# Two heads on 96 neighbouring partitions, and unit 1's gap rows sent by ScalarE

## The chip, the cores and the metric

The kernel runs on one core of a Trainium2 chip. The core has TensorE (PE, matrix products, with weight loads shown as PEld), VectorE (DVE), ScalarE (ACT), GpSimd (POOL) and SyncE (SP), which here only issues transfers. Sixteen DMA engines move data between memory and the core's 128-partition on-chip memory. The metric is the device time of one execution in microseconds (us), as the median of several runs.

## The reference

Two computations follow each other. The first is a gated linear recurrence for 4 batches, 8 heads, 768 steps and a head size of 48:

```
f = 1 / (1 + exp(-f_logit))
for t in range(S):
    state = f[:, :, t, :, None] * state + einsum('bhd,bhe->bhde', k[:, :, t], v[:, :, t])
    y[:, :, t] = einsum('bhd,bhde->bhe', q[:, :, t], state)
```

Its result, with the 8 heads side by side (8 x 48 = 384 columns, 4 x 768 = 3072 tokens), goes through a two-layer network: `h = x @ w_in` (384 to 2048), `g = where(h > 0, h, exp(min(h, 0)) - 1)`, `out = g @ w_out` (2048 to 384). q, k, v and f_logit are float32; w_in and w_out come as 8-byte floating point numbers, so each of their elements is twice as large in memory and is turned into float32 on the chip.

## The kernel before

**Units, pairs and halves.** The 3072 tokens are cut into 12 units of 256, three per batch. q, k and f lie with head elements on partitions and tokens innermost. The 8 heads are 4 pairs; in each half of 64 partitions one head of the pair takes 48 partitions and 16 stay over. Before the change the 48 rows stand first in each half (partitions 0 to 47 and 64 to 111, `HALF`, L403) and the 16 over are behind them (48 to 63 and 112 to 127).

**Rows of the network.** The network wants its 384 input rows as three blocks of 128. Three pairs give 96 rows each; the fourth pair's 96 rows are cut into six strips of 16, which go into the 16 partitions over in each half of the three blocks: the gap rows. In unit 0 matrix products write them in place (`first_outputs`, L719, with the zero-padded tiles `padded_v` and `padded_s`). From unit 1 on `carried` (L693) copies the products to `xt` on ScalarE and sends the six strips to their places with six small transfers (L717), issued by SP. `fetch` (L500) lays w_in's rows to match: two transfers for the 48-row parts and two for the 16-row parts of each piece (L515, L516).

**Attention of a unit.** `load` (L417) issues f, k and q as two transfers each, one per half, and v as one. In unit 0 the second half's transfers are issued by ScalarE, the rest by SP. `blank` (L430) fills the tiles of the first two units beforehand, so that the partitions over hold neutral values. `gates` (ScalarE, GpSimd) and `decays` (L588: a scan and a reciprocal on VectorE and products on GpSimd, for each of the 4 pairs) turn f into products of decays and scale k and q. `transposed` turns k (TensorE, L616) and ScalarE copies it to `kn` (L620); `advance` (L660, matmul L668), `step` (L624, VectorE), `scores` (L637), `mask` (L653), `outputs` (L674) and `carried` follow for chunks of 64 tokens.

**Weights.** There are 16 pieces, 8 of w_in and 8 of w_out, fetched into 7 places in turn (`AHEAD`). Each goes through `split` (two VectorE instructions, L530 and L534), `lower` (ScalarE, L540, about 1.9 us) and `merge` (VectorE, L548), and `merge` issues the fetch for the place that it frees.

**Order.** Each engine's instructions stand in an order written out by hand (a manual schedule). The start is listed one call after another (L970 to L1013); from there a plan says at which step T of the network which part of the attention, which merge and which load is issued (`at_step`, L760; the numbers `A1`, `D2`, `A2`, `D3`, `A3`). An even step T is one block of first-layer products (`up`, L864, psH) and an odd one a block of second-layer products, two blocks behind (`down`, L894, psM). `warm` (L961) puts products whose result nobody uses (psW) on TensorE at fixed places. The units from 2 on use a scheme with seven products in place of eight for 2 by 2 blocks (L819, L916), with sums on GpSimd (L883).

**Queues.** Transfers start in the order in which SP or ScalarE issues them, and up to eight completion counters are used in turn by all of them, whichever engine issues.

## Time and profile before

| | |
|---|---|
| Median of 14 runs | 578.52 us (576.31 to 579.71) |
| The profiled execution, its own time | 578.4 us |
| Its span | 576.7 us |
| Mean granted clock of TensorE | 0.987 |
| TensorE busy | 556.1 us (96%) |
| VectorE busy | 437.0 us (76%) |
| ScalarE busy | 235.3 us (41%) |
| GpSimd busy | 271.0 us (47%) |
| DMA queue of SP | 36144 packets, 49.07 MB |
| DMA queue of ScalarE | 912 packets, 0.79 MB |

The profile is of one execution. The views used below: the chain of work that ended last (start, duration, what), the timeline of an engine (start, busy time, engine, line, operation, tile written and read, how many; in brackets how long the engine stood before it, and for what), the transfers by queue (packets, MB, share of the DMA engines) and the view by stretches of time (stretch and its length; busy time and number of instructions of PE, PEld, DVE, ACT and POOL; then the granted clock of TensorE, the busy share of the DMA engines, and GB/s). All times are counted from the start of the span. L with a number is a line of the kernel.

### The profile page before, as it was taken

What the parts mean: (1) busy time and instruction counts of PE and PEld (TensorE: products, weight loads), DVE (VectorE), ACT (ScalarE), POOL (GpSimd) and SP (SyncE); (2) the same over time, 40 slices, a digit from 0 to 9 for tenths busy, and PEclk for the clock granted to TensorE, in tenths of its full rate; (3) what the DMA queues carried; (4) which work ended last, traced back from release to release, by engine and by line L of the source; (5) the groups of instructions that cost most, each with busy time, mean ns of one, the idle gap of its engine ahead of it and who ended that gap; (6) DMA issues with size and microseconds to landing.
All of it is one profiled execution on the core that took longest, in us unless ns stands there. A gap on an engine that the chain in (4) does not pass through costs nothing.

```text
span 576.7 us, 15424 instructions
## 1 busy us (share of the span) xinstructions
PE 556.1 (96%) x6236; PEld 505.4 (88%) x6236; DVE 437.0 (76%) x838; ACT 235.3 (41%) x437; POOL 271.0 (47%) x559
## 2 busy tenths in 40 slices
PE   6599999999999999999999999999999999999994
PEld 2376777777999999999999999999999999999994
DVE  7799659674896896897897887788878888745542
ACT  3357855443433343343343343443343253343331
POOL 6320014851466366267257257356357348325332
PEclk9979999999999999999999999999999999999998
DMA  8999980034014216216206207207207201201001
GB/s 180 231 237 266 191 221 0 2 83 90 2 42 109 81 42 131 84 30 145 84 15 159 85 8 166 84 8 167 83 7 168 85 3 60 84 2 35 28 2 34
DMA packets 37138, 50.94 MB, mean 88 GB/s; under 512 B 4257, under 2 KB 27841, under 8 KB 37057
## 3 DMA queue, kind: packets, MB, share of 16 engines
q1 hardware_dynamic: 36144, 49.07, 35.6%
q8 instruction: 51, 0.84, 0.6%
q10 hardware_dynamic: 912, 0.79, 0.6%
q14 instruction: 31, 0.25, 0.2%
HBM read 44.04 MB, written 4.72 MB: 85 GB/s over the span
## 4 chain that ended last, share of the span: by engine, by line
PE 89%; DVE 4%; issue 2%; ACT 1%; DMA 1%; POOL 1%; DVEq 0%; ACTq 0%; POOLq 0%
PE psH L819 32%; PE psM L916 31%; PE psH L864 7%; PE psM L894 7%; PE psS L647 3%; PE psY L684 2%; PE psY L704 2%; PE psW L965 2%; PE psT L616 2%; PE psU_a L668 1%; PE psY L743 1%; DVE o L926 1%; DMA f<-in_f_logit_dram 1%; DVE state L631 1%; DVE u L926 1%
## 5 line engine op out<-in xcount | busy, mean ns | idle before, releaser
L819 PE MATMUL psH<-xt,wi 128*128 128x128 f32 (+1 forms) x960 | 177.3, 294 | 0.0
L883 POOL TENSOR_TENSOR sums<-gg 128x128 f32<-128x128 f32 x160 | 69.7, 456 | 180.6 <-DVE gg L873 142.2
L851 ACT ACTIVATE gg<-hh 128x512 f32<-128x512 f32 x80 | 50.5, 631 | 223.9 <-POOL sums L883 130.9
L819 PEld LDWEIGHTS psH<-xt,wi 128*128 128x128 f32 x960 | 136.0, 192 | 0.7
L819 PE MATMUL psH<-xt,area 128*128 128x128 f32 x640 | 110.7, 275 | 0.0
L819 PEld LDWEIGHTS psH<-xt,area 128*128 128x128 f32 x640 | 96.9, 192 | 4.0
L916 PE MATMUL psM<-area,sums 128*128 128x192 f32 x480 | 91.1, 326 | 0.0
L828 DVE TENSOR_TENSOR hh<-psH,u 128x256 f32<-128x256 f32 x80 | 33.6, 420 | 68.8 <-ACT u L826 68.8
L597 DVE RECIPROCAL p<-f 128x256 f32<-128x256 f32 x48 | 84.1, 1753 | 1.7
L916 PEld LDWEIGHTS psM<-area,sums 128*128 128x128 f32 x480 | 80.2, 190 | 0.0
L916 PE MATMUL psM<-wo,gg 128*128 128x192 f32 x320 | 68.2, 336 | 0.0
L852 ACT ACTIVATE gg<-gg 128x512 f32<-128x512 f32 x96 | 60.6, 631 | 3.0
L873 DVE SCALAR_TENSOR_TENSOR gg<-gg,hh 128x512 f32<-128x512 f32 x80 | 56.5, 706 | 1.5 <-ACT gg L852 1.5
L916 PEld LDWEIGHTS psM<-wo,gg 128*128 128x128 f32 x320 | 50.2, 191 | 1.9
L841 DVE TENSOR_TENSOR hh<-psH,u43h 128x256 f32<-128x256 f32 (+1 forms) x160 | 49.7, 352 | 2.7
L598 POOL TENSOR_TENSOR k<-k,f 128x256 f32<-128x256 f32 x48 | 35.5, 740 | 28.3 <-DVE f L594 21.7
L883 POOL TENSOR_TENSOR sums<-gg,sums 128x128 f32<-128x128 f32 x80 | 43.4, 543 | 6.3
L864 PE MATMUL psH<-xt,wi 128*128 128x256 f32 x192 | 45.0, 385 | 0.7 <-DMA xt<-xt 0.7
L894 PE MATMUL psM<-wo,gg 128*128 128x384 f32 x128 | 44.2, 489 | 0.0
L864 PEld LDWEIGHTS psH<-xt,wi 128*128 128x128 f32 x192 | 36.3, 193 | 8.6 <-issue 2.3
L883 POOL TENSOR_TENSOR sums<-sums,gg 128x128 f32<-128x128 f32 x80 | 40.0, 500 | 0.0
L841 DVE TENSOR_TENSOR u43h<-psH,hh 128x256 f32<-128x256 f32 x80 | 33.5, 419 | 7.7 <-PE psH L819 7.7
(96 smaller groups left out, 752.8 us busy)
## 6 DMA issues: line engine op xcount, KB each, us to landing
area<-in_moe_w_out_dram SPq DMA_DIRECT2D x8, 768.0 KB, 8.2
again<-in_moe_w_in_dram SPq DMA_DIRECT2D x16, 384.0 KB, 4.2
again<-in_moe_w_out_dram SPq DMA_DIRECT2D x16, 384.0 KB, 3.7
v<-in_v_dram SPq DMA_DIRECT2D x12, 384.0 KB, 7.5
area<-in_moe_w_in_dram SPq DMA_DIRECT2D x16, 288.0 KB, 8.9
f<-in_f_logit_dram SPq DMA_DIRECT2D x23, 192.0 KB, 4.7
k<-in_k_dram SPq DMA_DIRECT2D x23, 192.0 KB, 5.6
q<-in_q_dram SPq DMA_DIRECT2D x23, 192.0 KB, 7.1
```

The lines of the kernel that those rows point to most:

```text
L597: nc.vector.reciprocal(pts[u][:, p], g)
L598: nc.gpsimd.tensor_tensor(out=t["k"][:, p], in0=t["k"][:, p], in1=g, op=ALU.mult)
L819: nc.tensor.matmul(to, lhsT=lhs, rhs=rhs, start=(n == 0), stop=True, skip_group_check=True)
L828: add = lambda to, x, y: nc.vector.tensor_tensor(out=to, in0=x, in1=y, op=ALU.add)
L841: add = lambda to, x, y: nc.vector.tensor_tensor(out=to, in0=x, in1=y, op=ALU.add)
L851: nc.scalar.activation(g[:], h, AF.Relu, scale=-1.0)
L852: nc.scalar.activation(g[:], g[:], AF.Exp, scale=-1.0)
L864: nc.tensor.matmul(ph[:, i], lhsT=wi[j][:, kt, i * 128 : (i + 1) * 128], rhs=xts[m][:, kt, :], start=(kt == 0), stop=(kt == NKT - 1),)
L873: nc.vector.scalar_tensor_tensor(out=g[:], in0=g[:], scalar=-1.0, in1=phs.pop(P), op0=ALU.add, op1=ALU.max)
L883: nc.gpsimd.tensor_tensor(out=s[:, i], in0=x, in1=y, op=op)
L894: nc.tensor.matmul(pm[t][:], lhsT=g[:, i, t * 128 : (t + 1) * 128], rhs=wo[:, 2 * j + i, :], start=(j == 0 and i == 0), stop=(j == NP - 1 ...
L916: nc.tensor.matmul(pm[bank][:, half * DH : (half + 1) * DH], lhsT=x, rhs=y, start=first, stop=(j == NP - 1), skip_group_check=True,)
```

## The change

The two heads of a pair now lie on the neighbouring partitions 16 to 111 (`MAIN`); the 16 partitions over are 0 to 15 and 112 to 127 (`GAP`).

- f, k and q of a unit come in one transfer each on 96 partitions, all issued by SP, also in unit 0. The 96-row part of each w_in piece is one transfer; its two 16-row parts stay separate.
- v gets 16 columns of zeros in front as well as behind, and each state is kept in strips of 64, the first 16 of which are zero, in five fixed tiles. Products that read a half now read all its 64 rows, and those that write a half write 64 rows, with the zeros falling on the 16 partitions over. `even_v` is a copy of half of unit 0's v, padded in the same way, for `first_outputs`; `padded_v` and `padded_s` grow from 32 to 48 columns per strip. GpSimd clears the new tiles and makes the copy.
- The tile `at` has one buffer instead of two.
- The six gap-row transfers of unit 1 are issued by ScalarE, those of later units by SP as before.

```diff
+    MAIN = slice(PAD, 64 + D)
+    GAP = (0, 64 + D)
...
-    vs = [cst.tile([128, NW, DM + PAD], FP32, name=f"v{i}") for i in range(NB)]
+    vs = [cst.tile([128, NW, PAD + DM + PAD], FP32, name=f"v{i}") for i in range(NB)]
...
-            for r in range(2):
-                ((other or nc.sync) if r else nc.sync).dma_start(
-                    out=qkf[u % NB][n][HALF[r]],
-                    in_=src[n][b, r::2, :, s0 : s0 + U].rearrange("p d s -> d p s"),
-                )
+            nc.sync.dma_start(
+                out=qkf[u % NB][n][MAIN],
+                in_=src[n][b, :, :, s0 : s0 + U].rearrange("(p r) d s -> (r d) p s", r=2),
+            )
...
+    def of_head(u, b, w, r, p):
+
+        frm = (2 * p + r) * D + r * PAD
+        return vs[u % NB][FULL[b], w, frm : frm + 64]
...
-    load(0, nc.scalar)
+    load(0)
...
-        nc.gpsimd.memset(vs[i][:, :, DM:], 0.0)
-
-    padded_v = cst.tile([128, NW, 2 * NKT, 2 * PAD], FP32, name="padded_v")
+        for frm in (0, PAD + DM):
+            nc.gpsimd.memset(vs[i][:, :, frm : frm + PAD], 0.0)
+
+    boxes = [cst.tile([128, (HP + 1) * 64], FP32, name=f"state{i}") for i in range(5)]
+    for box in boxes:
+        nc.gpsimd.memset(box[:].rearrange("n (p d) -> n p d", d=64)[:, :, 0:PAD], 0.0)
+
+
+    even_v = cst.tile([128, NW, NKT, 64], FP32, name="even_v")
+    nc.gpsimd.memset(even_v[:], 0.0)
+    padded_v = cst.tile([128, NW, 2 * NKT, 3 * PAD], FP32, name="padded_v")
     nc.gpsimd.memset(padded_v[:], 0.0)
-    padded_s = cst.tile([128, NC - 1, NKT, 2 * PAD], FP32, name="padded_s")
+    padded_s = cst.tile([128, NC - 1, NKT, 3 * PAD], FP32, name="padded_s")
...
-        main = w_in[0 : NKT * 2 * D, c].rearrange("(k r d) f -> r d k f", r=2, d=D)
+        nc.sync.dma_start(out=to[MAIN], in_=w_in[0 : NKT * 2 * D, c].rearrange("(k q) f -> q k f", k=NKT))
         rest = w_in[NKT * 2 * D :, c].rearrange("(r k d) f -> r d k f", r=2, d=PAD)
         for r in range(2):
-            nc.sync.dma_start(out=to[64 * r : 64 * r + D], in_=main[r])
-            nc.sync.dma_start(out=to[64 * r + D : 64 * r + 64], in_=rest[r])
+            nc.sync.dma_start(out=to[GAP[r] : GAP[r] + PAD], in_=rest[r])
...
-        s = sb.tile([128, HP, D], FP32, tag="state", name=f"state{u}_{c}", bufs=5)
+        box = boxes[(u * NC + c) % len(boxes)]
+        s = box[:].rearrange("n (p d) -> n p d", d=64)[:, 0:HP, PAD:]
...
-        at = ats[u] = sb.tile([128, 2, NW, HP, C], FP32, tag="at", name=f"at{u}")
+        at = ats[u] = sb.tile([128, 2, NW, HP, C], FP32, tag="at", name=f"at{u}", bufs=1)
...
-                            pc[r][FULL[b], w, p], lhsT=t["k"][HALF[r], p, cols], rhs=t["q"][HALF[r], p, cols],
+                            pc[r][FULL[b], w, p], lhsT=t["k"][FULL[r], p, cols], rhs=t["q"][FULL[r], p, cols],
...
-                            py[b][HALF[r ^ b], w, p], lhsT=sts[u, c][HALF[r], p],
-                            rhs=t["q"][HALF[r], p, c * C : (c + 1) * C],
+                            py[b][FULL[r ^ b], w, p], lhsT=sts[u, c][FULL[r], 64 * p + r * PAD : 64 * (p + 1) + r * PAD],
+                            rhs=t["q"][FULL[r], p, c * C : (c + 1) * C],
...
-            frm, g = 64 * r + j * PAD, 64 * r + D
-            nc.sync.dma_start(out=x[g : g + PAD, j, :], in_=x[frm : frm + PAD, NKT, :])
+            frm, g = (1 - r) * PAD + 64 * r + j * PAD, GAP[r]
+            (nc.sync if u > 1 else nc.scalar).dma_start(out=x[g : g + PAD, j, :], in_=x[frm : frm + PAD, NKT, :])
...
+    nc.gpsimd.tensor_copy(
+        even_v[:, :, :, PAD:],
+        vs[0][:, :, PAD : PAD + NKT * 2 * D].rearrange("t w (p r d) -> t w p r d", r=2, d=D)[:, :, :, 0],
+    )
```

## The prediction

> **What bounds the kernel now.** I read the chain of work that ended last, in order of time, first, because TensorE is busy for 96% of the span and the question is only where it is not.

> ```profile
> 1.56 3.91 DMA f<-in_f_logit_dram
> ...
> 21.55 6.16 issue
> ...
> 39.66 2.59 PE psH L864 x12
> 42.25 3.43 PE psW L965 x8
> 45.69 1.08 PE psU_a L668 x64
> ```

> From 45.69 us on this chain is TensorE work piece after piece; what lies ahead of it is the start, and there the chain holds a transfer (3.91 us) and a pause of 6.16 us in which TensorE waits for nothing that the profile shows. It is in the middle of 48 equal matmuls (L743, 15 before it, 33 after), so no data is missing. The trace records transfers of instructions on a queue of their own:

> ```profile
> q8 instruction: 51, 0.84, 0.6%
> ```

> That is 16 KB a packet. I read the pause as TensorE out of instructions while the packet stands behind data[...]. That is an inference.

> The same start seen from VectorE, in the timeline:

> ```profile
> 26.22 0.56 DVE L530 TENSOR_SCALAR bits<-area 128x768 int32<-128x768 int32 x1 [3.03 <-DMA area<-in_moe_w_in_dram]
> ...
> 35.70 0.96 DVE L548 CUSTOM_DVE_ANT_0 wi<-area,bits 128x1536 uint16<-128x1536 uint16 x1 [0.52 <-ACT area L540]
> ```

> VectorE works through the weight's split and unit 1's decays in a fixed order; at 23.2 it comes to the split of the second w_in piece, which has not landed, and stands 3.03 us. Everything after that is a VectorE queue without a gap (9.3 of 10 us busy from 30 to 50), and TensorE's transposes of unit 1 (L616, k of pair 3 ready at 39.12) and the kn copies (ready at 44.59) hang on it. So two waits for transfers run side by side, and the one on VectorE decides what comes later: TensorE fills 42.25 to 45.68 with matmuls on ident whose result nobody reads (psW).

> How fast the transfers are, in the view by stretches (last two columns: share of the DMA engines, GB/s; the one before is the granted clock):

> ```profile
> 28.00:36.00 8.00, 7.57 (x109) 4.95 (x101) 7.36 (x9) 3.68 (x6) 3.55 (x5) 0.50 1.06 231
> ...
> 40.00:50.00 10.00, 9.82 (x100) 6.63 (x98) 9.31 (x21) 9.69 (x10) 0.00 (x0) 1.00 1.06 203
> 50.00:54.00 4.00, 4.00 (x78) 2.60 (x82) 3.93 (x7) 2.45 (x3) 0.00 (x0) 1.00 1.02 372
> ```

> The engines are full in all three rows, but move 203 GB/s where w_in's pieces on 48 and 16 partitions are under way and 372 where w_out's on 128 are. The transfers are slow for their shape, not for want of requests.

> Last, the only later stop that a transfer causes on TensorE, and SP's side of it, in the timeline:

> ```profile
> 67.53 4.38 SPq L717 DMA_DIRECT2D xt<-xt  x6
> ...
> 72.75 2.83 PE L864 MATMUL psH<-xt,wi 128*128 128x256 f32 x12 [0.70 <-DMA xt<-xt]
> ```

> ScalarE had finished the copies at 62.56, but SP issued the six gap transfers only from 67.53, behind w_in's fetches.

> **Part 1: one transfer on 96 partitions for f, k, q and w_in's main rows.** Same bytes and rows, fewer issues (7 to 4 per unit, 4 to 3 per w_in piece, 0.31 to 0.46 us each on SP, which is not on the path). What counts is the rate. Row: 203 GB/s with 48 partitions, 372 with 128.[...] I take 300, between the two rows[...].

> Up to the second w_in piece 2 x 1536 KB of unit loads and 2 x 768 KB of w_in move, 4.72 MB. At 300 GB/s from about 3 us that ends at 18.7, landing near 20; by the bare row of 128 partitions (372) 15.7; at 203 as today, 26.2. VectorE comes to it at 23.2, so above 4.72/(23.2 - 4) = 246 GB/s the 3.03 us are gone whole: -3.03 (0 to -3.03). The 0.52 us at 35.2 goes too (-0.52, 0 to -0.52): there VectorE waits for ScalarE's L540, which starts at 33.74 behind copies of TensorE's result, and TensorE's pause should end earlier. Its instructions came at 27.71, 1.5 us after the w_in piece had landed, so they stood behind the same data[...], and with the data through by 19 to 20 I put their arrival at 22.5 (21.5 to 24).

> The first f: 3.91 us from issue to landing, in two queues at 160 to 234 GB/s; f alone first in one queue, 393 KB at 300, is 1.3 us of data plus the rest: -0.3 (0 to -0.6). It carries through ScalarE, VectorE and the GpSimd chain to 17.2.

> After that VectorE and GpSimd have the same work. The second half of the transposes ends at 39.66 - 3.55 = 36.1 (with the +0.3 of part 2), psH 2.59, psW 3.43, psU at 42.1. kn, at 44.59 - 3.55 = 41.0, is ready by then. If TensorE's pause alone went and VectorE's wait did not, TensorE would stand before the transposes instead.

> **The clock.** With the pause shortened, TensorE comes to unit 1's transposes early: instructions at 22.5, then the 33 left of L743 at full clock (44 took 0.87, so 20 ns each: 0.7), the between copies (0.43), the 72 of part 1 (1.45), psW (4 x 0.43), psH (2.6): 29.4, the first transposes to 29.7, and it idles until k of pair 3, at 39.12 - 3.55 = 35.6. The row: after the idle from 21.55 the clock was 0.50 in 28 to 36 (from 26.4 to 36.7 counting the neighbouring stretches).[...] It speaks against this change: the idle moves from ahead of small matmuls, whose slowness was hidden, to right ahead of psH and psW, 6 us of dense work on the path. By the row, a repeat of 10.2 us at half speed costs up to 5.1[...]; I take +1.0 (0 to +2.5; beyond it is rival a).

> **Part 2: what the layout adds.** GpSimd clears more: by its rows (384 elements 0.42, 288 in 0.34, so 0.83 ns each and 0.1 fixed) two more v strips 0.18, five state strips 0.83, even_v 0.42, the longer padded tiles 0.28: 1.71 us, from 4.71 to 6.42. Its next work is at 7.23: hidden; without that 0.8 us of slack each us is on GpSimd's chain. The copy into even_v (288 elements; nearest, padded_v's 192 in 0.67) is 1.0 us, 17.8 to 18.8, and TensorE wants it at 19.72: hidden by the masks. Beside it runs VectorE's split of piece 0, whose first half took 1.09 beside GpSimd against 0.56 elsewhere: +0.3 (0 to +1.0), carried on by merge and steps. Matmuls over 64 rows instead of 48, and 64 columns instead of 48: L684 (64 by 64) took 217 ns and L704 (48 by 48) 217 too: nothing. State in strips of 48 at a step of 64: the same 192 elements, 357 ns: nothing. One at tile instead of two: the mask of unit 1 (52.25) follows the last reader of unit 0's (by 28.8) by 23 us: nothing.

> **Part 3: unit 1's gap rows from ScalarE.** Six issues of about 0.4 (its three at the start took 0.37 to 0.42), 2.4 us after the copies at 62.56 (by then 59), landing 2 to 5 us on, so by 66; TensorE wants them near 69. The stop goes: -0.70 (0 to -0.70). Queued behind on ScalarE is L540, whose merge ends at 65.5 and is used by psM at 69.31: 3.8 us of slack cover 2.4; the later ones have 5.9 and 7.1. On SP, later loads share completion counters with these six, so the loads of unit 2 can wait for them; the w_in piece behind is split at 79.91, some 15 us later: hidden.

> **Sum.** -0.3 - 3.03 - 0.52 + 0.3 + 1.0 - 0.70 = -3.25. From the profiled 578.4 (576.7 of span) that is 575.15; the median of the runs is 578.52, 0.1 higher, so 575.3. From 150 us on TensorE is busy 418.75 of 420 and nothing moves.

> **Rivals.** (a) The clock dip eats most of it: +4.0 instead of +1.0, 578.3; at +3.0, 577.3. For: a whole dip of 10.2 us is in the trace.[...] (b) The rate does not rise, being set by row length or the reading side: no -0.3, -3.03 nor -0.52, and the clock as before: 578.5 - 0.7 + 0.3 = 578.1, or 577.5 where the copies' +0.3 falls into VectorE's wait and the f does gain. Against: w_out shows 372. (c) Slower: ScalarE's issues stand in its queue waiting for earlier transfers to land (w_in's took 8.5 to 8.9 us in the median), holding L540 and the exponentials behind. 3.8 us are free, and 4.25 more eat the gains without the dip: above 8 us of holding it is slower; at 10, merge 9 is 6.2 late and the time 578.5 - 4.25 + 6.2 = 580.5. Against: in the built program only the last two issues wait for earlier transfers, w_out pieces that SP had issued by 51.5 us.

> **How the numbers follow.** The forecast 0.76, (a) 0.12, (b) 0.07, (c) 0.05. Best end of the forecast: all of 0.6 + 3.03 + 0.52 + 0.70 with no dip, 573.7; the runs of before spread 1.7 around their middle, so 572.0. The upper end takes in (b) and most of (a): 578.3. No change means within 0.2% (1.16 us), about what the spread of runs lets one tell. Faster than 577.36: nearly all of the forecast, half of (a) and (b), 0.85; same 0.09; slower 0.06.

> **What would show it.** VectorE's wait at L530 for w_in near 23 us gone; 280 GB/s and more between 5 and 20 us; TensorE's pause in L743 under 3 us; psU of unit 1 near 42 to 44; no wait for xt at the twelfth step. The clock row tells the dip: 0.50 shortly after 30 to 35 us. It is wrong if the rate stays near 210, or if ScalarE's L540 after the six issues starts 8 us late.

## The result

The changed kernel takes 574.76 us (median of 10 runs, 574.38 to 576.01). The kernel before, run beside it and with its earlier runs counted in, takes 579.27 us (median of 47, 576.31 to 583.67). The ratio is 0.9923, with a 95% interval of 0.9905 to 0.9941: 4.5 us, or 0.8%, faster. Forecast were 575.3 us and a gain of 3.25. The runs also spread less: their standard deviation is 0.5 us, against 1.5 before.

The profiled execution of the changed kernel took 575.79 us, with a span of 574.0 and a mean granted clock of 0.991. That is 1.0 above the median, while the profiled execution of before (578.4) lies 0.9 below its own. So the two traces differ by only 2.6 us, and the start is read in its own times below, not from the ends.

In the lines below psT are the transposes of k, psU the products of `advance`, psS the scores and psY the outputs.

The chain of work that ended last (start, duration, what):

```profile
1.56 4.15 DMA f<-in_f_logit_dram
...
21.79 2.97 issue
...
26.31 3.03 PE psY L760 x65
...
30.79 1.95 ACT area L552
32.76 0.07 DVE wi L560
...
47.11 1.15 PE psS L660 x62
48.27 2.78 PE psM L910 x8
```

The pause in which TensorE waits for nothing visible fell from 6.16 to 2.97 us. From there the chain goes over TensorE's products and ScalarE's `lower` (L552) to VectorE's merge (L560), and along VectorE to the scores at 47.11. The first f did not come earlier: 4.15 us instead of 3.91.

The timeline of VectorE and TensorE:

```profile
23.38 0.56 DVE L542 TENSOR_SCALAR bits<-area 128x768 int32<-128x768 int32 x1
24.76 1.12 PE L760 MATMUL psY<-at,padded_v 64*32 64x64 f32 x33 [2.97 <-issue]
32.76 0.96 DVE L560 CUSTOM_DVE_ANT_0 wi<-area,bits 128x1536 uint16<-128x1536 uint16 x1 [0.32 <-ACT area L552]
36.24 0.44 PE L628 MATMUL psT<-ident,k 128*128 128x128 f32 x2 [0.87 <-POOL k L610]
42.63 1.15 PE L681 MATMUL psU_a<-v,kn 64*64 64x48 f32 x64
```

The split of the second w_in piece starts at 23.38 with no wait; before, it started at 26.22 after one of 3.03. The psU matmuls of unit 1 start at 42.63, 3.0 us earlier than before:

```profile
45.62 1.15 PE L668 MATMUL psU_a<-v,kn 64*64 64x48 f32 x64
```

The wait went narrowly. By the trace's records of landings, the last part of that piece landed at 23.26, 0.12 us ahead of the split. In four more traces whose start is the same (runs 5 to 8) it landed at 22.08 to 22.81, 0.4 to 1.1 us ahead.

The view by stretches (before the GB/s: granted clock and share of the DMA engines), of the changed kernel and then of the first two stretches before:

```profile
4.00:12.00 8.00, 7.54 (x14) 2.62 (x12) 5.72 (x10) 2.70 (x6) 5.58 (x20) 1.00 1.11 251
12.00:18.00 6.00, 4.93 (x16) 2.23 (x16) 5.86 (x7) 0.59 (x1) 6.00 (x8) 1.00 1.14 229
...
24.00:28.00 4.00, 2.81 (x75) 2.45 (x77) 3.93 (x5) 0.33 (x2) 1.31 (x5) 0.54 0.97 287
28.00:34.00 6.00, 6.00 (x50) 4.08 (x47) 5.61 (x8) 3.36 (x4) 2.48 (x4) 0.74 1.05 255
34.00:40.00 6.00, 5.13 (x27) 3.98 (x26) 5.86 (x10) 4.24 (x4) 1.41 (x2) 1.00 1.06 250
```

```profile
4.00:12.00 8.00, 6.75 (x14) 2.38 (x12) 5.93 (x11) 2.70 (x6) 4.53 (x12) 1.00 1.11 230
12.00:18.00 6.00, 5.18 (x30) 2.47 (x33) 5.90 (x6) 0.71 (x2) 5.83 (x8) 1.00 1.12 201
```

So from 4 to 18 us 96-row transfers run at 251 and 229 GB/s where there were 230 and 201, and not at the 300 taken. This trace is the slowest of its kind: in the eight others whose f, k, q and w_in come in 96 rows the same stretches moved 259 to 268 and 243 to 271. The half clock lasts from 24.3 to 31.1 us, on the small matmuls after the pause and the psW behind them; before, it lasted from 26.1 to 36.4.

ScalarE and VectorE at the gap rows of unit 1, and TensorE at the twelfth step:

```profile
59.12 4.04 ACTq L729 DMA_DIRECT2D xt<-xt  x6
63.21 1.92 ACT L552 ACTIVATE area<-area 128x768 uint16<-128x768 uint32 x1 [3.52 <-issue]
65.16 0.96 DVE L560 CUSTOM_DVE_ANT_0 wo<-area,bits 128x1536 uint16<-128x1536 uint16 x1 [6.10 <-ACT area L552]
...
66.45 2.74 PE L910 MATMUL psM<-wo,gg 128*128 128x384 f32 x8
...
69.03 2.75 PE L880 MATMUL psH<-xt,wi 128*128 128x256 f32 x12
```

The stop for xt is gone: psH starts at 69.03 instead of 72.75, which makes 3.72 us with what was gained before. But the six issues take 4.04 us, and ScalarE's next work starts 3.52 us behind its copies, not 2.4. The merge behind it ends at 66.12, only 0.33 us before psM uses its result. The last gap row landed at 68.87, 0.16 us before psH, where 66 was forecast. From there to the end the lead in the two traces shrinks from 3.7 to 2.7 us with no wait that stands out.

### The profile page after: what moved, and what is told of

The parts are those of the page before. It is cut to its first block, busy times and chain, and to the rows that moved or that the text cites. A ratio compares the mean times of both kernels' runs of the same rounds, so it can differ in the third digit from the quotient of the medians.

```text
span 574.0 us, 15339 instructions
## 1 busy us (share of the span) xinstructions
PE 556.6 (97%) x6236; PEld 505.7 (88%) x6236; DVE 436.9 (76%) x838; ACT 235.3 (41%) x437; POOL 273.5 (48%) x568
## 3 DMA queue, kind: packets, MB, share of 16 engines
HBM read 44.04 MB, written 4.72 MB: 85 GB/s over the span
## 4 chain that ended last, share of the span: by engine, by line
PE 82%; DVE 10%; ACT 3%; issue 3%; POOL 1%; DMA 1%; DVEq 0%; ACTq 0%; POOLq 0%
PE psH L835 29%; PE psM L932 29%; PE psM L910 7%; PE psH L880 6%; PE psS L660 2%; PE psY L716 2%; PE psY L696 2%; PE psT L628 1%; PE psU_a L681 1%; DVE state L644 1%; DVE hh L857 1%; DVE state L647 1%; PE psY L760 1%; DVE o L942 1%; DVE p L609 1%
```

## The experiments

Unless said otherwise each kernel is the changed one with one edit. The kernel before was run beside them: 579.41 us with runs 1, 4, 5 and 8, 579.23 with runs 2, 3, 6 and 7, 579.13 with 9 and 10, and 580.12 with 11 and 12. Ratios are to it; with their intervals they are estimated from all runs, and are not always the quotient of the two medians (in run 4 that is 0.9983).

**1. The 96 rows again as two transfers of 48** (layout, state strips and gap rows stay as changed).

```diff
-            nc.sync.dma_start(
-                out=qkf[u % NB][n][MAIN],
-                in_=src[n][b, :, :, s0 : s0 + U].rearrange("(p r) d s -> (r d) p s", r=2),
-            )
+            for r in range(2):
+                nc.sync.dma_start(
+                    out=qkf[u % NB][n][PAD + r * D : PAD + (r + 1) * D],
+                    in_=src[n][b, r::2, :, s0 : s0 + U].rearrange("p d s -> d p s"),
+                )
...
-        nc.sync.dma_start(out=to[MAIN], in_=w_in[0 : NKT * 2 * D, c].rearrange("(k q) f -> q k f", k=NKT))
+        main = w_in[0 : NKT * 2 * D, c].rearrange("(k r d) f -> r d k f", r=2, d=D)
...
+            nc.sync.dma_start(out=to[PAD + r * D : PAD + (r + 1) * D], in_=main[r])
```

> The changed kernel with its new layout, but each transfer on 96 partitions (f, k, q, and w_in's main rows) sent as two of 48, all by SP. Theory (the rate of a transfer on 96 partitions removed VectorE's wait for the second w_in piece): the rate between 12 and 18 us falls from 229 back to about 200 GB/s, VectorE waits 2 to 3 us again before the split of that piece, TensorE's pause in the first outputs grows from 2.97 to 5 us or more, and the time is 577.3 to 577.8. Rival (the layout or the order of the instructions gave the gain): no wait, 574.8 as the changed kernel.

Measured: 580.14 us, ratio 1.0013 (0.9994 to 1.0032). The whole gain is lost, and the time is 2.3 us above the range expected. Timeline and stretches:

```profile
27.97 1.17 PE L762 MATMUL psY<-at,padded_v 64*32 64x64 f32 x33 [6.26 <-issue]
28.69 0.56 DVE L544 TENSOR_SCALAR bits<-area 128x768 int32<-128x768 int32 x1 [5.34 <-DMA area<-in_moe_w_in_dram]
...
12.00:18.00 6.00, 5.02 (x20) 2.31 (x23) 5.86 (x7) 0.59 (x1) 6.00 (x9) 1.00 1.12 176
...
40.00:46.00 6.00, 5.02 (x16) 3.97 (x17) 5.83 (x10) 3.98 (x4) 1.42 (x2) 0.72 1.06 231
```

Both waits are back and larger than before the change, and the rate is 176 GB/s where one transfer gave 229. That it is also below the 201 of the kernel before, which had two transfers too, on other partitions, stays unexplained. In addition the clock fell to 0.72 in the stretch of unit 1's psH, which took 4.44 us instead of 2.76.

One transfer for two is also fewer transfers, so the gain could come from their number. Against that, the DMA engines are full in both (shares of 1.12 and 1.14), and each packet takes longer: by the packet records from 4 to 18 us, a 1024-byte packet of the unit loads took 93 to 101 ns in the mean here, 80 to 89 before and 77 to 81 in the changed kernel. What in the path of a packet is slower for 48 rows is not shown.

**2 and 3. Only f, k and q in halves, and only w_in's main rows in halves** (each half of edit 1 alone).

> The changed kernel with the unit loads f, k and q as two transfers of 48 rows each, w_in's main rows still as one of 96. All of it split again gave 580.1. Ahead of the second w_in piece 2.36 MB of unit loads and 1.18 MB of w_in's main rows move. Theory A (each byte costs by the rows of its transfer, whichever tensor it is): two thirds of the delay come back, the data end near 26 us instead of 22.2, VectorE stands 2.5 to 3 us for that piece, the time is 577.5 to 578.5. Theory B (it is w_in's transfers that slow the queue): VectorE's wait is under 1 us and the time 575 to 576.

> The changed kernel with w_in's main rows as two transfers of 48 rows each, f, k and q still as one of 96. Theory A (bytes and rows alone): a third of the delay, the data end near 24 us, VectorE stands 0.5 to 1 us for the second w_in piece, the time is 575.3 to 576.3. Theory B (w_in's transfers slow the queue): VectorE stands 3 us or more and the time is 578 or more.

Measured: 578.72 us (0.9976 to 1.0019) for f, k and q; 578.21 us (ratio 0.9976, 0.9958 to 0.9995) for w_in. VectorE's split of the second piece, first with f, k and q in halves, then with w_in:

```profile
27.36 0.56 DVE L543 TENSOR_SCALAR bits<-area 128x768 int32<-128x768 int32 x1 [3.85 <-DMA area<-in_moe_w_in_dram]
```

```profile
24.55 0.56 DVE L543 TENSOR_SCALAR bits<-area 128x768 int32<-128x768 int32 x1 [1.33 <-DMA area<-in_moe_w_in_dram]
```

The waits, 3.85 and 1.33, add up to 5.18, near the 5.34 of both together. Both tensors' transfers cost by their rows, and neither alone. The waits stand at 2.9 to 1, where the bytes (2.36 and 1.18 MB) stand at 2 to 1, and both are larger than expected. The first time lies 0.2 us above its range. The second looks like a clear miss (expected 575.3 to 576.3) until run 6: 2 us of it lie behind the last output and have another cause. Without them it would be 576.2.

**4. The kernel before, with unit 1's v issued behind the second w_in piece**: 393 KB less ahead of the piece that VectorE waits for, all rows as before. `load_v` holds the transfer of v, which `load` calls for all other units.

```diff
     load(1)
     fetch(1)
+    load_v(1)
```

> The kernel before, with only the transfer of unit 1's v issued behind the second w_in piece instead of ahead of it (393 KB less ahead of that piece; at 201 GB/s 1.9 us). Theory (VectorE's wait for the second w_in piece decides): that wait falls from 3.03 to about 1.1 us, TensorE's pause in the first outputs stays about 6 us, and the time falls by 1.5 to 2, to 577.3 to 577.8. Rival (TensorE's pause decides): the time stays at 579.3.

Measured: 578.41 us, ratio 1.0006 (0.9979 to 1.0033). The interval leaves room for a gain of 1.2 us, not for the 1.5 to 2 expected. VectorE:

```profile
24.59 0.56 DVE L535 TENSOR_SCALAR bits<-area 128x768 int32<-128x768 int32 x1 [1.36 <-DMA area<-in_moe_w_in_dram]
...
35.12 0.96 DVE L553 CUSTOM_DVE_ANT_0 wi<-area,bits 128x1536 uint16<-128x1536 uint16 x1 [1.58 <-ACT area L545]
```

The wait for the piece fell by 1.67 us, the wait of the merge for ScalarE grew from 0.52 to 1.58, and psU came only 0.6 earlier (45.00). TensorE's pause, 5.6 us there instead of 6.16, delays its products; ScalarE copies those ahead of its `lower`, and the merge needs `lower`. The merge had waited for ScalarE before too, by the 0.52, so this way already ended last, and VectorE's wait for the piece lay beside it. To shorten only VectorE's brings at most a part of it; the change shortened both.

**5. The gap rows of unit 1 from SP, as those of the other units.**

```diff
-            (nc.sync if u > 1 else nc.scalar).dma_start(out=x[g : g + PAD, j, :], in_=x[frm : frm + PAD, NKT, :])
+            nc.sync.dma_start(out=x[g : g + PAD, j, :], in_=x[frm : frm + PAD, NKT, :])
```

> The changed kernel with unit 1's gap rows sent by SP again. Theory (part 3 is worth the stop of 0.70 us at the twelfth step): the stop is back, 0.5 to 1.0 us, time 575.3 to 575.8, and ScalarE no longer stands 3.5 us before its next lower step. Rival (ScalarE's six issues cost as much as they save): time 574.8 or less.

Measured: 577.63 us, ratio 0.9971 (0.9955 to 0.9987): 2.9 us slower than the changed kernel, where 0.5 to 1.0 was expected. And the trace shows no stop for xt:

```profile
59.37 6.99 SPq L729 DMA_DIRECT2D xt<-xt  x6
...
68.39 2.75 PE L880 MATMUL psH<-xt,wi 128*128 128x256 f32 x12
```

SP, with fewer issues ahead of it, begins the gap rows at 59.37 instead of 67.53. The last one landed at 67.56, 0.83 us before TensorE uses it: earlier than ScalarE's did in the changed kernel. So in these traces the stop goes by part 1 of the change, without part 3.

It shows another loss. From the last packet of the output to the last instruction it takes 5.4 us, against 3.4 in the changed kernel, and 1.04 us of that is SP standing after its 352nd recorded instruction.

**6. Six more transfers from SP that nobody needs**, with the gap rows left to ScalarE.

```diff
+        for i in range(2 * NKT if u == 1 else 0):
+            r, j = divmod(i, NKT)
+            frm = (1 - r) * PAD + 64 * r + j * PAD
+            nc.sync.dma_start(out=spare[frm : frm + PAD], in_=x[frm : frm + PAD, NKT, :])
```

> The changed kernel, with six more 16 KB transfers issued by SyncE into a tile that nobody reads, straight behind unit 1's gap rows, which ScalarE goes on sending. SyncE's program is then as long as in the kernel whose gap rows all go from SyncE (358 instructions instead of 350), and TensorE waits for nothing new. That kernel lost 2.9 us and its profile showed no late gap row, but 2.0 us more between the landing of the last output and the end of the program, in SyncE's closing instructions[...]. Theory A (the loss is how SyncE's closing instructions are delivered, and has nothing to do with the gap rows): 576.5 to 577.5, and 5.0 to 5.5 us from the last output's landing to the end instead of 3.4. Theory B (the loss is the gap rows' own lateness or ScalarE's queue used for the first time at the end): 574.8, and 3.4 us at the end.

Measured: 576.58 us, ratio 0.9954 (0.9938 to 0.9970). From the instruction records of the traces (SP's recorded instructions; us from the last output packet to the end; SP's stand after instruction 352, where there is one):

```
before                              420   3.5   none
changed                             350   3.4   none
all in halves (1)                   415   3.4   none
f, k, q in halves (2)               407   4.1   none
w_in in halves (3)                  359   5.5   1.07
gap rows from SP (5)                358   5.4   1.04
six more transfers from SP (6)      358   5.6   0.97
six more transfers from ScalarE (7) 350   3.8   none
```

The loss belongs to the length of SP's program, not to the gap rows. Where SP's closing instructions run past the 352nd, it stands 1 us there, and from the last output packet to the end it takes 5.4 to 5.6 us, against 3.2 to 4.3 in all the others of this study. Where the program is 407 or longer that instruction lies earlier, under other work. That a packet of instructions is fetched there is inferred. Runs 5 and 6 have the same tail and still differ by 1.05 us. That may be what the gap rows from ScalarE are worth (0.70 was forecast), but no trace shows where: TensorE ends at 565.50 us in run 5's trace and at 565.56 in run 6's. The trace of run 5 is of its fastest execution; its 20 runs fall into ten at 576.6 to 577.4 and ten at 577.9 to 579.2, and whether the slower ten have the stop stays open.

**7. The same six transfers from ScalarE instead**, behind unit 1's gap rows (the rest as in run 6).

```diff
+            nc.scalar.dma_start(out=spare[frm : frm + PAD], in_=x[frm : frm + PAD, NKT, :])
```

> The changed kernel, with six more 16 KB transfers issued by ScalarE into a tile that nobody reads, straight behind unit 1's gap rows: ScalarE's hold becomes 8 us instead of 4.04. The prediction's step gave ScalarE 3.8 us of slack and put the issues at 2.4 us. Theory A (slack as the profile after shows it: the merge that waits for ScalarE ends 0.3 us before TensorE needs it): four more us of hold make TensorE wait 3.5 to 4 us for that merge, and the time is 577.5 to 578.5. Theory B (there is slack elsewhere, for instance TensorE takes the wait out of a later one): below 576.

Measured: 582.28 us, ratio 1.0053 (1.0036 to 1.0070). TensorE's timeline, and its stretch:

```profile
71.79 5.41 PE L915 MATMUL psM<-wo,gg 128*128 128x384 f32 x8 [4.29 <-DVE wo L561]
...
70.00:76.00 6.00, 4.21 (x7) 2.39 (x8) 3.80 (x6) 4.77 (x6) 0.00 (x0) 0.51 1.06 263
```

The wait is the expected one: 4.70 us more hold, less 0.33 of slack, is 4.4; it is 4.29. But the time is 3.8 above the range's upper end, since behind the idle the granted clock was 0.51 (70 to 76 us): these 8 matmuls take 5.41 us instead of 2.74. 4.29 + 2.67 = 6.96, of the 7.5 that it lost. (The psH of unit 1 also took 4.44 us in this execution, after an idle of 2.16; more on that at the end.)

**8. Without the 8 matmuls on ident at step 4** (the psW ahead of psU; nobody reads them).

```diff
-    at_step(4, lambda: warm(4))
```

> The changed kernel without the four products on ident at step 4 (eight matmuls, 3.4 us on TensorE, whose result nobody reads). Theory (VectorE's queue decides the start up to the steps of unit 1): psU of unit 1 starts about 0.9 us earlier, near 41.7 us, when kn is copied, and TensorE waits that much longer before psS for VectorE's steps; time 574.8 within 0.4. Rival (TensorE's own work decides): 573.9. Rival (the idle lowers the granted clock, and psH pays): 576 or more.

Measured: 574.99 us, ratio 0.9935 (0.9908 to 0.9963), the same as the changed kernel. psU starts at 40.54 instead of 42.63, and then TensorE waits at the scores, in its timeline:

```profile
35.82 4.44 PE L880 MATMUL psH<-xt,wi 128*128 128x256 f32 x12
...
46.97 1.16 PE L660 MATMUL psS<-q,k 64*64 64x64 f32 x62 [0.60 <-DVE state L644]
```

Those start at 46.97, where the changed kernel has them at 47.11. VectorE's steps set the pace, as in the changed kernel, whose chain runs on VectorE from 32.76 us to the scores; even a psH at low clock (4.44 instead of 2.76) is covered. VectorE itself stood 0.60 us here for a piece of w_out.

**9. Three of the first seven products on ident left out**, each two matmuls (six fewer ahead of the pause).

```diff
-    warm(5)
+    warm(2)
```

> The changed kernel with three of the first matmuls on ident (psW) left out, each of which is two matmuls and two weight loads in the records: six pairs fewer ahead of the pause. Nobody reads them. Theory A (TensorE runs out of delivered instructions at a fixed count): the pause comes after 21 of the 48 padded_v matmuls instead of 15. Theory B (it waits for something that these matmuls need): it comes after 15 as before.

TensorE's timeline:

```profile
22.88 0.53 PE L760 MATMUL psY<-at,padded_v 64*32 64x64 f32 x21
...
24.02 0.63 PE L760 MATMUL psY<-at,padded_v 64*32 64x64 f32 x27 [0.61 <-issue]
```

The pause moved from after 15 to after 21 of the padded_v matmuls, six later, and so stayed at the same count of 221 matmuls. It has nothing to do with these matmuls' data. (One run, 578.11 us, so its time says little; the granted clock was 0.72 from 12 to 18 us, and everything came late.)

**10. Unit 1's v behind five more weight pieces** (`load_v` as in run 4, on the changed kernel).

```diff
     for n in range(2, AHEAD):
         fetch(n)
+    load_v(1)
```

> The changed kernel with unit 1's v (393 KB) issued behind the next five weight pieces instead of ahead of the second w_in piece; unit 1 needs it at 42 us only. Theory A (TensorE's pause in the padded_v matmuls is an instruction packet that stands behind queued data, and data queued at 231 to 250 GB/s is what it waits for): 393 KB less are 1.6 us, the packet starts near 20.6 instead of 22.18, TensorE goes on near 23.2 and the pause is 1.0 to 1.8 us instead of 2.97. Since VectorE decides by then (its split of the second piece started at 23.38 without a wait), the time stays within 0.6 of the changed kernel's 574.8. Theory B (the pause has nothing to do with the data that is queued): it stays at 2.5 to 3.

Measured: 580.15 us, ratio 1.0008 (0.9982 to 1.0034). TensorE's timeline and one stretch:

```profile
22.64 0.66 PE L765 MATMUL psY<-at,padded_v 64*32 64x64 f32 x33 [1.26 <-issue]
...
35.34 0.69 PE L633 MATMUL psT<-ident,k 128*128 128x128 f32 x2 [3.82 <-POOL k L615]
35.82 5.04 PE L885 MATMUL psH<-xt,wi 128*128 128x256 f32 x12
...
46.53 1.39 PE L686 MATMUL psU_a<-v,kn 64*64 64x48 f32 x64 [2.23 <-DMA v<-in_v_dram]
...
34.00:40.00 6.00, 4.67 (x12) 3.86 (x13) 5.83 (x10) 3.98 (x3) 1.42 (x2) 0.50 1.06 249
```

The pause shrank to 1.26 as theory A said, and the packet started at 20.1. The time missed by 5 us, and two reasons make up 4.5 of them. v came too late: issued at 33.98 behind the pieces, it cost 2.23 us of wait. And TensorE, being earlier, idled 3.82 us ahead of its last transposes, whereupon psH ran at a granted clock of 0.50 and took 2.28 us longer.

**11. v behind one more piece only.**

```diff
     for n in range(2, AHEAD):
         fetch(n)
+        if n == 2:
+            load_v(1)
```

> The changed kernel with unit 1's v behind one further weight piece (the third) instead of behind five. The run with v behind five shortened TensorE's pause from 2.97 to 1.26 us as expected, but then TensorE stood 3.8 us for k ahead of the last transposes, the granted clock of the next stretch was 0.50, 12 psH matmuls took 5.04 us instead of 2.76, and v itself landed 2.2 us late. Here v lands before 35 us, so the clock alone is left. Theory A (the clock dip on psH costs what the prediction gave it, about 1 us): a pause of 1.0 to 1.8 us, 4 us of idle before the last transposes, psH at half clock, the psU matmuls at 43.3 to 44.0 instead of 42.63, 575.3 to 576.2. Theory B (the dip is covered): 574.5 to 575.1.

Measured: 576.74 us, ratio 0.9949 (0.9931 to 0.9967), above the range of either theory. The pause was 1.53 us, there was no wait for v, and TensorE idled 3.01 us before the transposes; yet in the profiled execution the clock stayed at 1.00 from 28 us, psH took 2.76 and psU came at 41.86. That execution took 575.13. The 19 runs fall into two groups, four at 574.8 to 575.6 and fifteen at 576.4 to 577.6. Eleven of the fifteen have a mean clock of 0.989 to 0.992 against 0.994 to 0.995 in the four, but the other four of the fifteen have 0.994 to 0.995 too. So the clock may explain most of the 1.9 us, not all; the rest is open.

**12. As 11, with the 8 matmuls on ident put between the halves of unit 1's transposes** instead of ahead of psU.

```diff
-        at_step(then[0], lambda: transposed(u, 0, "a0"), lambda: transposed(u, 1, "a1"))
+        at_step(then[0], lambda: transposed(u, 0, "a0"), lambda: warm(4 * (u == 1)), lambda: transposed(u, 1, "a1"))
...
-    at_step(4, lambda: warm(4))
```

> As the run with v behind one further piece, and the 8 matmuls on ident that keep TensorE busy ahead of the psU matmuls (warm at step 4) stand between the two halves of unit 1's transposes instead, where TensorE would idle. Theory A (the dip comes from that idle): no stretch under 0.9 between 34 and 46 us, psH in 2.8 us, the psU matmuls at 40.5 to 41.2. Then either VectorE's steps are the floor (the scores matmuls at 47 as in the changed kernel, 574.4 to 575.0), or they are not and the time falls by up to 1.5, to 573.3. Theory B (the dip comes whatever TensorE does there): psH takes over 4 us.

Measured: 574.82 us, ratio 0.9913 (0.9882 to 0.9943). 1.22 us of idle are left, psH takes 2.75 and psU begins at 40.61. Then, in TensorE's timeline:

```profile
42.16 4.54 PE L885 MATMUL psH<-xt,wi 128*128 128x256 f32 x12
46.64 1.16 PE L665 MATMUL psS<-q,k 64*64 64x64 f32 x64
```

The idle moved to the wait for kn ahead of psU (1.95 us) and the low clock to the psH behind it, so theory A held for the first psH only. VectorE's steps end at 46.76 there, where the scores begin at 46.64, so there is little that an earlier TensorE could still gain. The time is the changed kernel's, which agrees with VectorE's steps as the floor. No version tried beats it.

## Why the prediction was right, point by point

- **Rows of a transfer.** Right in kind, wrong in size. Runs 1 to 3 show that the 96-row transfers are the gain. The rate taken, 300 GB/s, was too high: 229 to 251 up to 18 us in this trace, at most 271 in any with 96 rows throughout, and the sign of 280 and more did not show. The second w_in piece landed at 23.26 us, where about 20 was forecast; 4.72 MB by then are 245 GB/s by the prediction's own division, next to the 246 above which the wait was to vanish. That the wait went whole in this trace is luck, by 0.12 us. The 300 was the author's estimate between the rows of 203 and 372; the nearest row was the 203 of 48-row transfers, and it should have weighed more.
- **-3.03 and -0.52.** The first went whole, of the second 0.32 is left. But "the one on VectorE decides what comes later" is the step that failed. Run 4 took 1.67 of it away, and psU came 0.6 earlier, as much as TensorE's pause shrank: the merge's wait for ScalarE ended last, and what ScalarE waits for is TensorE's products after its pause. The sum held because the same data release both. That 0.32 is left comes from TensorE's instructions at 24.76 and not 22.5: the rate, again.
- **TensorE out of instructions.** Runs 9 and 10 bear it out: the pause came after the same 221 matmuls, and shrank from 2.97 to 1.26 us when 393 KB less were queued. The packet records agree: in all 14 traces TensorE goes on 1.2 to 1.6 us after a packet of 16 KB on the instruction queue has ended (before: 26.25 and 27.71; changed: 23.31 and 24.76). That the packet carries TensorE's instructions is inferred.
- **-0.3 for the first f.** Wrong: in the changed kernel it landed 0.24 us later. Over the ten kernels with one transfer for f it takes 3.73 to 4.15 us, against 3.91 and 3.95 in the two with f on two queues: no difference beyond the spread.
- **+0.3 for the copy beside VectorE.** It did not show: the first half of the split took 1.08 us beside GpSimd as it had before (1.09).
- **+1.0 for the clock.** The +1.0 was the author's estimate. In the trace the clock cost nothing: the pause was long enough to keep TensorE's idle ahead of the transposes at 0.87 us and not the 5.9 worked out. The dip is real: with the pause at 1.26 (run 10) psH ran at a granted clock of 0.50 and took 2.3 us longer. That is rival (a), kept away by the slower transfers, and not always: of the five traces with this start (the changed kernel and runs 5 to 8) two, runs 7 and 8, have this psH at 4.44 us. How often the changed kernel's own runs have it is not shown.
- **-0.70 for the stop at the twelfth step.** It went, but by the trace of run 5 it goes with SP's issues too, so the term belongs to part 1 as much as to part 3. Run 5 against run 6 puts part 3 at 1.05, with no cause to be seen. ScalarE's slack of 3.8 us was read rightly; the issues held its next work back by 3.5 of them, not 2.4, and left 0.3. Rival (c) was nearer than it looked: in run 7 the issues take 8.7 us, over the 8 us from which the rival was to decide, and that kernel is indeed slower than before. It takes 582.3, where that working gives 578.5 - 4.25 + 4.9 = 579.2; the working had left out the clock.
- **The sum.** -3.0 by 42 us and -3.7 by 73 in the trace, against -3.85 and -4.55 forecast without the clock and the copy, or -2.55 and -3.25 with them. So two losses that did not come about made up for the f and for the part of the wait that stayed: that the total came so near is partly luck. The traces differ by 2.6 us at the end and the medians by 4.5; the 1.9 between is the two profiled executions' place among their runs, and with a spread of 1.5 us before, one trace of each can't say more.

## What to carry to other kernels

Two transfers of 48 partitions that become one of 96 raised the start's rate, with the same bytes, from 201 to 230 GB/s before to 229 to 271 in the nine traces of such kernels, and the gain lies where VectorE, in its fixed order, reaches the data (a wait of 3.03 us before, none after). Ask what else is behind the same queue: here, as inferred from runs 9 and 10, TensorE's instructions were, and their delay reached VectorE through ScalarE (run 4: the merge's wait of 1.58 us). Before a part of a change is judged by a variant's time, look at the time after the last output too; here 2 us (3.4 against 5.4 to 5.6) came and went with the length of a program that only issues transfers.

## What the runs showed of the hardware that was not expected

```profile
32.62:36.04 3.42, 1.26 (x10) 0.99 (x9) 3.35 (x5) 3.02 (x3) 1.20 (x2) 1.00 1.10 185
36.04:39.45 3.41, 3.41 (x10) 2.70 (x9) 3.34 (x7) 1.39 (x2) 0.22 (x1) 0.50 1.04 285
```

```profile
30.89:34.30 3.41, 1.57 (x11) 1.17 (x9) 3.38 (x5) 1.45 (x3) 0.94 (x2) 1.00 1.06 295
34.30:37.72 3.42, 2.25 (x12) 2.02 (x13) 3.32 (x6) 1.71 (x1) 1.43 (x2) 1.00 1.05 236
```
